# Moving the decay and value loads of units 5 to 11 from SP's queue to GpSimd's, with newly ordered engines

## The chip, the cores and the metric

The kernel runs on one core of one Trainium2 chip. The metric is the device time in microseconds (us) of one execution; the figure quoted is the median over runs. A core has five engines with an in-order instruction queue each: TensorE (PE, matmuls), VectorE (DVE), ScalarE (ACT), GpSimd (POOL) and SyncE (SP, which here only issues DMA transfers). Sixteen DMA engines move the data that the queues of SP and GpSimd ask for.

## The reference

A gated linear attention with a state per head, followed by a dense block with squared ReLU (cut to what matters):

```python
# q, k, v, alpha: (B=4, H=8, S=768, D=48) float32; alpha in [0.8, 1.0)
state = zeros(B, H, D, D)
for t in range(S):
    state = alpha[:, :, t, :, None] * state + einsum('bhd,bhe->bhde', k[:, :, t], v[:, :, t])
    y[:, :, t] = einsum('bhd,bhde->bhe', q[:, :, t], state)
x = y.transpose(0, 2, 1, 3).reshape(3072, 384)
h = x @ w_in                  # (384, 2048)
g = maximum(h, 0) ** 2
out = g @ w_out               # (2048, 384), float32
```

## The kernel before

**Tiling.** The 768 steps of each of the 4 sequences are cut into chunks of T = 256 tokens. A *unit* g is one chunk of one sequence; there are 12, ordered chunk by chunk (units 0 to 3 are the first chunks of the four sequences, 4 to 7 the second, 8 to 11 the last). A chunk's 256 tokens lie on 128 partitions, two neighbouring tokens (j = 0, 1) in a row.

**One unit's steps**, by the names that the order tables use:

- `lda ldk ldq ldv`: four loads of 384 KB (decay alpha, keys, queries, values) into one of four RAW slots (g mod 4); a load waits until the readers of the slot's part have finished with the unit four before.
- `pr` (product of the two tokens' decays, tile prd), `ln` (its logarithm, tile lab), `m1i` (TensorE: running sums over the tokens), `ei` and `ea` (exponentials for keys, ek, and queries, eq), `ec` (decay of the whole chunk, acm), `bk` (the keys' factor of the first token). For units 2 and 3, `m1s`, `es` and `aq` give the queries' factor of the first token; from unit 4 on `lm` (a logarithm of alpha), `lb` (a difference) and `es` do.
- `ekm`, `eqm0`, `eqm1`: keys and queries times their factors (tile qks). `vc`: values cast to bf16 (tile vbf).
- `tr0`, `tr1`: transposes of qks into kqt, on TensorE with copies `et0`, `et1` for units 0 to 2, as DMA transposes issued by SP from unit 3 on.
- `p0`: scores and the new state on TensorE; `mk0`, `mk1` mask the scores (tile pm); `sa`, `sc`, `sd` update the state; `y`: the unit's output; `xe`, `xf` copy it out of PSUM (xbf); `xt` transposes it (TensorE for units 0 to 3, a DMA transpose from SP from unit 4 on).
- Dense block: `s1_g_u` (u = 0 to 7, each 6 matmuls of 256 columns: two pieces of the hidden layer), `re` (ReLU into rr), `sq` (square into gt), `s2_g_j_n` (4 matmuls of 384 columns, n = 0 to 3, for the tokens j), `oe` (copy out of PSUM), `out` (store from SP).
- `win0/1`, `wout0/1`: the weights, loaded by GpSimd's queue at the start. In TensorE's table `+512` and `+256` are filler matmuls on zeros ahead of the first dense work.

**What sets the order.** Nothing is decided while the kernel runs. TABLES holds, for each engine, the complete order of its steps as text; `arrange` assigns each named step to the engine in whose table it stands (many steps can run on two engines, given as `alts`), and `place` puts in the semaphore waits that the dependences need. An engine works its list strictly in order: a step that waits holds all behind it. The same holds for the DMA issues, which stand as steps in the lists of SP and GpSimd. The priorities, costs and due times (FRONT, ATTN, DENSE, P) in the code went into the search that made the tables; in the run they set nothing.

**Around the change.** `load(g)` (line 445) makes the four loads of a unit. POOL_LOADS (line 313) names the loads that go through GpSimd's queue; the rest go through SP's. AFTER (line 1060) holds the loads of the start back: lda2 waits for ldv1, wout0 for ldv1, the loads of unit 3 for wout0.

```python
if nm in POOL_LOADS.get(g, ""):
    ring, cost = "pool", 930
...
load_op[g, nm] = add(ring, lambda e, dst=dst, src=src: e.dma_start(dst, src), cost, ...,
    writes=[key], name=f"ld{nm}{g}", dma=f"{nm}{r}{ring}", lag=1230,
    after=([load_op[gate]] if gate else []))
```

The semaphore of a load is named by kind, slot and ring. Two first-layer groups share two PSUM banks in turn, so that `s1_g_u` waits for the `re` of two groups before; the second layer has one bank, so that the groups of one j wait for the `oe` of the other.

Of the kernel before, what the change touches and what calls it, by code (L numbers as in the profile page):

```python
# [204 lines left out]

TABLES = {
    "act": """
        table ln0_0 ln1_0 ei0_0 xcaus ea0_0 ei1_0 ea1_0 ec1_0 et00_0 ec0_0 vc0 ln1 et01_0 et11_0 ei1 ea1 xe0 xv0
        ec1 vc1 sa1 re0_0 re0_1 sq0_1 re0_3 xe1 re0_4 re0_5 ln2 re0_6 sq0_6 ei2 ea2 ec2 vc2 re1_2 es2 re1_3
        re1_4 et0_2 sq1_3 re1_6 sa2 sq1_6 oe0_0 ln3 ei3 ea3 ec3 oe0_1 es3 xf2 xe2 lm4 ln4 vc3 ei4 ea4 ec4 re2_0  # L210
        re2_1 es4 oe1_0 re2_2 re2_3 re2_4 re2_5 sa3 sq2_5 lm5 re2_7 ln5 re2_6 xe3 ei5 ea5 ec5 xv3 es5 oe2_0
        re3_0 oe2_1 lm6 re3_1 xe4 ln6 re3_4 re3_3 ei6 ea6 ec6 re3_6 sq3_5 re3_7 sq3_7 es6 re4_0 re4_1 re4_2
        re4_3 vc6 xe5 lm7 ln7 re4_7 oe3_1 re4_4 ei7 ea7 ec7 re4_6 sq4_6 es7 oe4_0 re5_0 re5_1 lm8 ln8 xe6 re5_2
        re5_3 ei8 ea8 re5_4 re5_5 es8 re5_6 re5_7 sq5_7 re6_0 re6_1 re6_2 vc8 oe5_0 xe7 lm9 ln9 re6_5 re6_6
        oe5_1 re6_7 ei9 ea9 es9 oe6_0 vc9 re7_0 lm10 re7_1 ln10 xe8 re7_3 ei10 ea10 re7_4 re7_5 es10 re7_6 re7_7
        re8_0 oe7_0 re8_1 re8_2 lm11 ln11 xe9 re8_3 re8_4 ei11 ea11 re8_5 re8_6 sq8_5 es11 sq8_7 re9_0 oe8_0
        vc11 re9_1 oe8_1 xe10 re9_3 re9_4 re9_5 re9_6 re9_7 re10_0 oe9_0 re10_1 re10_2 xe11 oe9_1 re10_3 re10_4
# [4 lines left out]
        zero zlinc zlstr zident zcaus zcaus1 zla0 zla1 zones zown zown0 zown1 zqk0 zqk1 zqk2 zlb0 zlb1 ekm0_0
        eqm0_0 ekm1_0 eqm1_0 et10_0 mk0_0 sa0 mk1_0 ekm1 eqm0_1 eqm1_1 sc0 et0_1 et1_1 mk1_1 mk0_1 sc1 re0_2 xf1
        sq0_3 pr2 xv1 sq0_5 re0_7 re1_0 re1_1 ekm2 sq0_7 aq2 eqm0_2 eqm1_2 re1_5 et1_2 sq1_1 sq1_5 re1_7 mk1_2
        pr3 sq1_7 sc2 mk0_2 bk3 eqm1_3 ekm3 aq3 pr4 eqm0_3 xv2 bk4 lb4 ekm4 eqm1_4 eqm0_4 sq2_1 mk1_3 mk0_3 sc3
        oe1_1 sd3 sq2_7 sq2_6 xf3 lb5 ekm5 eqm1_5 eqm0_5 sa4 mk1_4 mk0_4 re3_2 pr6 sc4 sq3_1 xf4 sq3_3 re3_5
        sq3_6 lb6 ekm6 sa5 mk0_5 sc5 mk1_5 eqm0_6 eqm1_6 oe3_0 xf5 sq4_1 re4_5 pr7 sq4_3 sq4_7 sq4_5 bk7 lb7
        eqm0_7 sa6 eqm1_7 ekm7 sc6 sd6 mk0_6 mk1_6 pr8 oe4_1 xf6 sq5_3 bk8 lb8 ekm8 sq5_5 sq5_6 sa7 mk0_7 sc7
        mk1_7 eqm0_8 eqm1_8 sq6_1 re6_3 sd7 sq6_3 pr9 xf7 re6_4 sq6_5 sq6_6 sq6_7 bk9 lb9 ekm9 eqm0_9 eqm1_9
        mk0_8 sa8 mk1_8 oe6_1 pr10 sq7_1 xf8 re7_2 sq7_3 bk10 lb10 sq7_5 ekm10 sq7_6 sq7_7 sa9 mk0_9 eqm0_10  # L230
# [6 lines left out]
        +256 +256 tr01_0 p0_0 tr11_0 kv0 +512 +512 +512 +256 +256 p1_0 m11 +512 +256 y0 +512 +512 +256 tr0_1 xt0
        tr1_1 +512 +512 +512 +512 +512 +256 p0_1 s1_0_0 s1_0_1 s1_0_3 s1_0_2 y1 s1_0_4 s1_0_5 xt1 s1_0_6 s1_0_7
        m1i2 s1_1_0 s1_1_1 s1_1_2 m1s2 s1_1_3 s1_1_4 tr0_2 s1_1_6 s1_1_5 tr1_2 s2_0_0_0 s1_1_7 p0_2 s2_0_0_1
        s2_0_0_2 s2_0_0_3 s2_0_1_0 s2_0_1_1 m1i3 s2_0_1_2 s2_0_1_3 m1s3 y2 s2_1_0_0 s2_1_0_1 xt2 s2_1_0_2 m1i4  # L240
        s1_2_0 s1_2_1 s2_1_0_3 s1_2_2 s1_2_3 s2_1_1_0 s1_2_4 s2_1_1_1 s1_2_5 p0_3 s2_1_1_2 s1_2_6 s1_2_7
        s2_1_1_3 y3 m1i5 s2_2_0_0 s2_2_0_1 xt3 s2_2_0_2 s2_2_0_3 s1_3_0 p0_4 s2_2_1_0 s2_2_1_1 s2_2_1_2 s2_2_1_3
        s1_3_2 s1_3_1 y4 s1_3_4 s1_3_3 m1i6 s1_3_6 s1_3_5 s2_3_0_0 s2_3_0_1 s1_3_7 p0_5 s2_3_0_2 s1_4_0 s1_4_1
        s2_3_0_3 s1_4_2 s1_4_3 y5 s2_3_1_0 s1_4_5 s2_3_1_1 s2_3_1_2 s1_4_7 s2_3_1_3 s1_4_4 m1i7 s2_4_0_0 s1_4_6
        s2_4_0_1 s2_4_0_2 p0_6 s2_4_0_3 s1_5_1 s1_5_0 s2_4_1_0 s2_4_1_1 s1_5_2 s2_4_1_2 s2_4_1_3 y6 s1_5_3 m1i8
        s2_5_0_0 s1_5_4 s1_5_5 s2_5_0_1 s1_5_6 s1_5_7 p0_7 s2_5_0_2 s1_6_0 s1_6_1 s2_5_0_3 s1_6_2 s1_6_3 y7
        s1_6_4 s2_5_1_0 s2_5_1_1 s1_6_5 s2_5_1_2 s1_6_6 s2_5_1_3 s1_6_7 m1i9 s2_6_0_0 s2_6_0_1 s2_6_0_2 s2_6_0_3
        s1_7_0 p0_8 s2_6_1_0 s2_6_1_1 s2_6_1_2 s2_6_1_3 s1_7_1 y8 s1_7_2 s1_7_3 m1i10 s2_7_0_0 s1_7_4 s1_7_5
        s2_7_0_1 s1_7_6 s1_7_7 s2_7_0_2 p0_9 s2_7_0_3 s1_8_0 s1_8_1 s1_8_2 s2_7_1_0 s2_7_1_1 s2_7_1_2 s2_7_1_3
        y9 m1i11 s1_8_3 s1_8_4 s2_8_0_0 s1_8_5 s1_8_6 s2_8_0_1 s1_8_7 p0_10 s2_8_0_2 s1_9_0 s2_8_0_3 s1_9_1  # L250
        s1_9_2 s2_8_1_0 s2_8_1_1 s2_8_1_2 y10 s2_8_1_3 s1_9_3 s1_9_4 s2_9_0_0 s1_9_5 s1_9_6 s2_9_0_1 s1_9_7
# [863 lines left out]
```

## Time and profile before

| | before |
|---|---|
| median of 3 runs | 174.28 us (173.72 to 176.34) |
| span of the profiled execution, first to last instruction | 171.8 us |
| TensorE matmuls, weight loads | 165.6 us (96%), 128.9 us (75%) |
| VectorE, ScalarE, GpSimd busy | 118.2 us (69%), 108.9 us (63%), 24.2 us (14%) |
| granted TensorE clock | 1.000 |
| DMA packets, bytes | 74743, 33.37 MB (194 GB/s over the span) |
| queue of SP (q1) and of GpSimd (q0), share of 16 engines | 73.6%, 12.4% |

The page gives no device time of the profiled execution other than its span; the median of the runs stands 2.5 us above it. Busy time of TensorE is modelled: matmuls are pipelined, and a busy TensorE can still be waiting between them. DMA issues do not count as busy time of the engine that issues them. A "busy tenths" row cuts the span into 40 slices of 4.3 us, one digit each.

### The profile page before, as it was taken

How to read it: one execution, taken by the hardware profiler on the slowest of the kernel's cores; microseconds unless marked ns; L12 is line 12 of the kernel's file. 1: busy time of each engine (PE TensorE's matmuls, PEld its weight loads, DVE VectorE, ACT ScalarE, POOL GpSimd, SP SyncE). 2: the span in 40 equal slices, each digit the busy share in tenths (PEclk: the TensorE clock that was granted, in tenths of full speed). 3: DMA queues.
4: the chain of work that ended last, by engine and by line, in shares of the span. 5: the costliest groups of instructions: out<-in, count | busy, mean ns of one | idle time of the engine just before them, and what ended most of it. 6: DMA issues, size and time to landing. Idle time of an engine off the chain costs nothing.

```text
span 171.8 us, 5397 instructions
## 1 busy us (share of the span) xinstructions
PE 165.6 (96%) x2377; PEld 128.9 (75%) x2377; DVE 118.2 (69%) x207; ACT 108.9 (63%) x210; POOL 24.2 (14%) x33
## 2 busy tenths in 40 slices
PE   7999999999999999999999999999999999999994
PEld 2556989766877787886768886787788788788773
DVE  5578789888756788975948986887959737432130
ACT  2958689658868278677359567475667464466440
POOL 4052712010252032100240000000420000000000
PEclk9999999999999999999999999999999999999999
DMA  5999999999999999998999998999999582050012
GB/s 143 323 298 186 260 316 219 245 245 288 182 234 209 269 173 211 305 217 146 288 168 211 267 192 153 337 178 243 255 211 205 81 103 85 0 141 0 22 69 92
DMA packets 74743, 33.37 MB, mean 194 GB/s; under 512 B 71648, under 2 KB 71904, under 8 KB 74720
## 3 DMA queue, kind: packets, MB, share of 16 engines
q1 hardware_dynamic: 73184, 28.32, 73.6%
q0 software_dynamic: 1536, 4.72, 12.4%
q8 instruction: 18, 0.29, 0.7%
q14 instruction: 5, 0.04, 0.1%
...
## 4 chain that ended last, share of the span: by engine, by line
PE 58%; DMA 20%; SPq 7%; DVE 6%; ACT 4%; POOL 2%; issue 2%; DVEq 0%
PE psWH L989 25%; PE psO L1035 24%; DMA raw<-in_alpha_dram 7%; DMA wout<-in_moe_w_out_dram 6%; DMA raw<-in_q_dram 4%; SPq L460 3%; DMA raw<-in_k_dram 3%; SPq L654 3%; PE psX L950 2%; POOL raw L460 2%; DVE pm L891 1%; PE psZ L762 1%; PE psX L874 1%; DVE qks L638 1%; DVE qks L643 1%
## 5 line engine op out<-in xcount | busy, mean ns | idle before, releaser
L989 PE MATMUL psWH<-xt,win 128*128 128x256 bf16 x552 | 70.9, 274 | 0.4 <-ACT rr L997 0.3
L989 PEld LDWEIGHTS psWH<-xt,win 128*128 128x128 bf16 x552 | 63.2, 144 | 5.2 <-ACT rr L997 1.1
L1035 PE MATMUL psO<-wout,gt 128*128 128x384 bf16 x352 | 66.7, 326 | 0.0
L997 ACT ACTIVATE rr<-psWH 128x512 bf16<-128x512 f32 x79 | 46.8, 597 | 24.4 <-PE psWH L989 22.9
L1035 PEld LDWEIGHTS psO<-wout,gt 128*128 128x128 bf16 x352 | 32.7, 98 | 16.7 <-DMA wout<-in_moe_w_out_dram 0.2
L1007 DVE TENSOR_TENSOR gt<-rr 128x1024 bf16<-128x1024 bf16 (+1 forms) x46 | 26.6, 584 | 22.0 <-ACT rr L997 21.9
L891 DVE TENSOR_TENSOR pm<-psZ,caus 128x1024 bf16<-128x1024 f32 x12 | 14.6, 1218 | 4.7 <-PE psWH L727 4.1
L1042 ACT ACTIVATE osb<-psO 128x384 f32<-128x384 f32 x17 | 8.3, 491 | 11.7 <-PE psO L1035 11.3
L891 DVE TENSOR_TENSOR pm<-psX,caus 128x1024 bf16<-128x1024 f32 x12 | 14.6, 1218 | 1.0 <-PE psX L874 0.5
L1010 POOL TENSOR_TENSOR gt<-rr 128x1024 bf16<-128x1024 bf16 x3 | 5.7, 1894 | 58.7 <-ACT rr L997 58.7
L643 DVE TENSOR_TENSOR qks<-raw,ek 128x768 bf16<-128x768 f32 x11 | 10.5, 952 | 3.0 <-DMA raw<-in_k_dram 2.5
L638 DVE TENSOR_TENSOR qks<-raw,eq 128x384 bf16<-128x384 f32 x22 | 11.4, 553 | 1.7 <-ACT eq L613 1.0
L1083 PE MATMUL psO<-zero 128*128 128x512 bf16 (+1 forms) x33 | 9.1, 407 | 1.3 <-DVE zero L382 1.3
L999 DVE TENSOR_SCALAR rr<-psWH 128x512 bf16<-128x512 f32 x13 | 8.9, 687 | 1.6 <-PE psWH L989 1.4
L1011 ACT ACTIVATE gt<-rr 128x512 bf16<-128x512 bf16 (+1 forms) x11 | 9.1, 823 | 0.7 <-DVE rr L999 0.4
L910 DVE CAST xbf<-psZ 128x384 bf16<-128x384 f32 x10 | 5.5, 554 | 3.2 <-PE psZ L754 3.2
L634 ACT ACTIVATE vbf<-raw 128x768 bf16<-128x768 f32 x7 | 5.9, 843 | 2.2 <-DMA raw<-in_v_dram 2.1
L567 DVE TENSOR_TENSOR prd<-raw 128x384 f32<-128x384 f32 x9 | 5.7, 636 | 2.1 <-DMA raw<-in_alpha_dram 2.0
L609 ACT ACTIVATE la<-raw 128x384 f32<-128x384 f32 x8 | 4.2, 524 | 4.5 <-DMA raw<-in_alpha_dram 4.5
L570 ACT ACTIVATE lab<-prd 128x384 bf16<-128x384 f32 x10 | 5.2, 521 | 2.4 <-DVE prd L567 2.3
L847 POOL TENSOR_TENSOR sbd<-tmp,acm 128x192 bf16<-128x192 f32 x5 | 2.9, 583 | 25.8 <-DVE tmp L837 22.7
L908 ACT ACTIVATE xbf<-psX 128x384 bf16<-128x384 f32 x11 | 5.3, 482 | 1.9 <-PE psZ L754 1.9
...
## 6 DMA issues: line engine op xcount, KB each, us to landing
raw<-in_alpha_dram SPq DMA_DIRECT2D x11, 384.0 KB, 5.9
raw<-in_k_dram SPq DMA_DIRECT2D x11, 384.0 KB, 5.8
raw<-in_q_dram SPq DMA_DIRECT2D x11, 384.0 KB, 5.0
raw<-in_v_dram SPq DMA_DIRECT2D x11, 384.0 KB, 5.0
out_dram<-osb SPq DMA_DIRECT2D x11, 384.0 KB, 3.4
win<-in_moe_w_in_dram POOLq DMA_DIRECT2D x2, 768.0 KB, 9.9
wout<-in_moe_w_out_dram POOLq DMA_DIRECT2D x2, 768.0 KB, 11.6
raw<-in_alpha_dram POOLq DMA_DIRECT2D x1, 384.0 KB, 11.1
```

What stands on the lines that cost most here:

```text
L460: load_op[g, nm] = add(ring, lambda e, dst=dst, src=src: e.dma_start(dst, src), cost, (L_PRIO[g] + j if ring == "sp" else W_PRIO[2] + 10 * ...
L638: add("dve", lambda e, j=j, dst=dst: e.tensor_tensor(dst, RAW[r][:, 2, :, j, :].rearrange("p (n x) d -> p n x d", x=2), EQ[la][:, j].rearr ...
L643: add("dve", lambda e, a=a, E=E: e.tensor_tensor(QKS[qs][:, a, :, :, 0:D], RAW[r][:, 1 + a].rearrange("p h j d -> p j h d"), E[la][:].rear ...
L891: add("dve", lambda e, hf=hf, psT=psT: e.tensor_tensor(PM[pm][:, hf].rearrange("p r n j t -> p (r n) (j t)"), psT[:, :, :].rearrange("p r ...
L989: ins = pe.matmul(psN[:, i * T:(i + 1) * T], WIN[:, kk, hidden(fj)], mov, start=(kk == 0), stop=(kk == KT - 1))
L997: add("act", lambda e, psN=psN, rr=rr: e.activation(rr, psN, AF.Relu), act_ns(512), pu + 600, reads=[keyN], writes=[("rr", rb, half)], nam ...
L999: alts={"dve": (lambda e, psN=psN, rr=rr: e.tensor_scalar(rr, psN, 0.0, None, ALU.max), dve_ns(512))})
L1007: add("dve", lambda e, dst=dst, sq=sq: e.tensor_tensor(dst, sq, sq, ALU.mult), 148 + k * 267, pu + 1200, reads=[("rr", rb, h) for h in ran ...
L1011: "act": (lambda e, dst=dst, sq=sq: e.activation(dst, sq, AF.Square), act_ns(k * 512))})
L1035: ins = pe.matmul(psS, GT[gt][:, fj, j, :], WOUT[:, fj, :], start=(fj == 0), stop=(fj == FT - 1))
L1042: add("act", lambda e, j=j, psS=psS: e.activation(OSB[ob][:, j], psS, AF.Copy), act_ns(DM), ps_ + 700, reads=[keyS], writes=[("osb", ob, j ...
L1083: pr.arrange(TABLES, lambda n: lambda pe: pe.matmul(psO[:, 0:n], ZERO[:, 0:128], ZERO[:, 0:n], skip_group_check=True), zero)
```

## The change

Loads of decays (a) and values (v) of units 5 to 11, 14 transfers of 384 KB, move from SP's list to GpSimd's. Keys and queries stay on SP. All five order tables are new. GpSimd's list grows from 29 to 59 steps, SP's shrinks from 84 to 70, ScalarE's from 210 to 193; VectorE's goes from 206 to 207 and TensorE's keeps its 276. Between the engines, 43 steps go from ScalarE to VectorE and 32 the other way (ReLUs, squares, copies out of PSUM), 18 from VectorE to GpSimd (pr2, pr3, pr4, pr6, pr8, pr10, pr11, bk3, bk8, bk9, bk11, aq3, sd3, sd7 and the squares sq1_5, sq7_5, sq10_3, sq11_3) and 8 back, 8 from ScalarE to GpSimd (vc1, vc3, vc6, vc9, vc11, sq0_6, sq2_5, sq8_5) and 2 back. No computation is added or removed.

```diff
-    POOL_LOADS = {2: "akqv"}
+    POOL_LOADS = {2: 'akqv', 5: 'av', 6: 'av', 7: 'av', 8: 'av', 9: 'av', 10: 'av', 11: 'av'}
```

The whole lists of GpSimd and SP, and of the others the parts that the text speaks of ("..." marks what is left out):

```diff
     "act": """
-        ... oe0_0 ln3 ei3 ea3 ec3 oe0_1 es3 xf2 xe2 lm4 ln4 vc3 ei4 ea4 ec4 ...
+        ... ln3 oe0_0 ei3 ea3 ec3 sq1_7 es3 lm4 xv2 ln4 oe0_1 ei4 re2_1 ea4 ec4 re2_3 vc5 es4 ...
     "dve": """
-        ... ekm2 sq0_7 aq2 eqm0_2 eqm1_2 re1_5 et1_2 ... pr3 sq1_7 sc2 mk0_2 bk3 eqm1_3 ekm3 aq3 pr4 eqm0_3 xv2 bk4 ...
+        ... ekm2 sq0_5 sq0_7 aq2 eqm0_2 eqm1_2 et0_2 re1_6 et1_2 re1_7 mk1_2 mk0_2 sc2 sq1_6 xe2 xf2 eqm0_3 eqm1_3 ekm3 re2_0 bk4 ...
-        ... xf5 sq4_1 re4_5 pr7 sq4_3 sq4_7 sq4_5 bk7 lb7 eqm0_7 sa6 eqm1_7 ekm7 ...
+        ... eqm0_6 sd5 eqm1_6 sq4_3 re4_5 pr9 lb7 bk7 sq4_5 re4_7 eqm1_7 ekm7 sa6 mk1_6 sc6 mk0_6 eqm0_7 ...
     "pe": """
-        ... s2_4_0_1 s2_4_0_2 p0_6 ... y6 s1_5_3 m1i8 ...
+        ... y4 m1i6 s1_3_4 s1_3_5 s2_3_0_0 s1_3_6 s1_3_7 s2_3_0_1 p0_5 s2_3_0_2 s2_3_0_3 s1_4_1 m1i7 s1_4_0 s1_4_3 y5
+        s2_3_1_0 s1_4_2 s2_3_1_1 s1_4_5 s2_3_1_2 s2_3_1_3 s1_4_4 s1_4_7 s2_4_0_0 s1_4_6 s2_4_0_1 s2_4_0_2 p0_6 ...
     "pool": """
-        slinc slstr sident scaus scaus1 win0 win1 lda2 sd0 ldq2 ldv2 ldk2 wout0 sd1 wout1 bk2 sd2 sq2_3 vc4 pr5
-        bk5 sd4 vc5 bk6 sd5 sq5_1 vc7 sq8_1 vc10
+        slinc sident scaus1 scaus slstr win0 win1 lda2 ldv2 vc1 ldk2 wout0 ldq2 sd0 pr2 wout1 sq0_6 sq1_5 ldv5
+        pr3 pr4 bk3 aq3 vc3 lda5 pr5 sq2_5 sd3 lda6 bk5 lda7 pr6 bk6 ldv6 lda8 vc6 pr8 lda9 lda11 lda10 ldv7 vc7
+        pr10 ldv8 bk8 pr11 bk9 ldv9 ldv10 ldv11 sd7 vc9 vc10 sq7_5 bk11 sq8_5 vc11 sq10_3 sq11_3
     "sp": """
-        lda0 ldk0 ldq0 ldv0 lda1 ldk1 ldv1 ldq1 lda3 ldk3 ldq3 lda4 ldv3 ldk4 ldq4 ldv4 tr0_3 tr1_3 lda5 tr0_4
-        out0_1 tr1_4 ldk5 ldq5 ldv5 lda6 ldk6 tr1_5 tr0_5 out2_1 xt4 ldq6 out1_1 ldv6 lda7 ldq7 ldk7 tr0_6 tr1_6
-        xt5 ldv7 out3_1 lda8 ldk8 tr0_7 tr1_7 out4_1 xt6 ldq8 ldv8 lda9 ldq9 ldk9 tr0_8 tr1_8 xt7 ldv9 lda10
-        out5_1 ldk10 tr0_9 tr1_9 out6_1 xt8 ldq10 ldv10 lda11 ldk11 tr0_10 tr1_10 out7_1 xt9 ldq11 ldv11 tr0_11
-        tr1_11 xt10 out8_1 xt11 out9_1 out10_1 out11_0 out11_10 out11_11
+        lda0 ldk0 ldq0 ldv0 lda1 ldk1 ldq1 ldv1 lda3 lda4 ldq3 ldk3 ldk4 ldv3 ldq4 tr1_3 tr0_3 ldk5 ldv4 tr0_4
+        tr1_4 out0_1 ldq5 ldk6 tr0_5 tr1_5 out1_1 xt4 ldq6 ldk7 ldq7 tr1_6 tr0_6 xt5 out2_1 ldk8 tr1_7 xt6 tr0_7
+        ldq8 out3_1 ldk9 ldq9 out4_1 tr1_8 xt7 tr0_8 ldk10 ldq10 out5_1 tr1_9 tr0_9 xt8 out6_1 ldk11 ldq11
+        tr0_10 tr1_10 xt9 tr1_11 out7_1 tr0_11 xt10 xt11 out9_1 out8_1 out11_0 out10_1 out11_10 out11_11
```

More of the change, by code (lines that the diff above doesn't have):

```diff
@@ L207 @@
     "act": """
[L208 to L217, printed above, removed]
@@ L220 @@
+        xe11 re10_3 re10_5 re10_4 re10_7 re10_6 re11_0 sq11_1 oe10_0 re11_2 oe10_1 re11_5 sq11_5 re11_7 oe11_0
+        oe11_11
     """,
     "dve": """
[L222 to L230, printed above, removed]
@@ L237 @@
[L237 to L246, printed above, removed]
@@ L247 @@
[L247 to L251, printed above, removed]
```

51 lines of the change are left out of this document (41 added, 10 removed).

## The prediction

> **What bounds the kernel now.** I read the busy times and the slices of the page first, then the chain of waits, then the timelines of TensorE, GpSimd and VectorE at the places that the change touches.
>
> ```profile
> span 171.8 us, 5397 instructions
> PE 165.6 (96%) x2377; PEld 128.9 (75%) x2377; DVE 118.2 (69%) x207; ACT 108.9 (63%) x210; POOL 24.2 (14%) x33
> PEclk9999999999999999999999999999999999999999
> DMA  5999999999999999998999998999999582050012
> ```
>
> TensorE is nearly never idle and its granted clock is full. The 16 DMA engines are as full as TensorE until slice 31 of 40 (about 130 us) and then nearly empty, so the first three quarters are a race of two full resources; GpSimd has 86% of its time free. A busy TensorE may still run with waits between pipelined matmuls, so I count its work. The dense layers, with the chain's pieces as their pace:
>
> ```profile
> L989 PE MATMUL psWH<-xt,win x552: 272/273/334, 18.1 to 164.6; 128*128 128x256 bf16 x184
> L1035 PE MATMUL psO<-wout,gt x352: 323/326/337, 30.9 to 166.5; 128*128 128x384 bf16 x176
> ```
>
> ```profile
> 81.29 6.32 DMA raw<-in_alpha_dram
> 87.62 0.57 DVE prd L567
> 88.22 0.53 ACT lab L570
> ...
> 91.20 0.65 PE psO L1035 x4
> 91.85 1.31 PE psWH L989 x12
> ...
> 166.81 2.65 PE psX L950 x32
> ```
>
> Undisturbed, a first-layer matmul takes 1.31/12 = 0.109 us and a second-layer one 0.65/4 = 0.163 us. By the code there are 576 of the one (12 units of 8 groups of 6) and 368 of the other ahead of the last 32: 62.9 + 59.8 + 2.65 = 125.4 us. TensorE's work runs from 18.1 us (first row, its first dense matmul) to 166.81 + 2.65 = 169.5 us, so 26.0 us are left for attention and waits. What an attention step costs, and what a wait looks like, stand in TensorE's timeline:
>
> ```profile
> 77.40 0.33 PE L576 MATMUL psWH<-lab,linc 128*128 128x384 bf16 x1
> ...
> 77.67 0.81 PE L1035 MATMUL psO<-wout,gt 128*128 128x384 bf16 x4
> ...
> 78.97 1.46 PE L1035 MATMUL psO<-wout,gt 128*128 128x384 bf16 x8
> 80.83 0.42 PE L874 MATMUL psX<-kqt 64*64 64x128 bf16 x16 [0.40 <-ACT eq L613]
> ...
> 81.65 0.82 PE L1035 MATMUL psO<-wout,gt 128*128 128x384 bf16 x4
> ...
> 86.97 0.37 PE L762 MATMUL psZ<-vbf,pm 64*128 64x48 bf16 x16
> ...
> 87.67 0.88 PE L989 MATMUL psWH<-xt,win 128*128 128x256 bf16 x6
> 88.80 0.34 PE L576 MATMUL psWH<-lab,linc 128*128 128x384 bf16 x1 [0.24 <-ACT lab L570]
> ```
>
> Start to start, the decay sums (m1i) take 0.27, the scores (p0) 0.82, the output (y) 0.70 us. After 18.1 us there are 10 m1i, 10 p0 and 11 y: 2.7 + 8.2 + 7.7 = 18.6 us; the 34 transposing matmuls of 128 columns for units 1 to 3 add 34 x 0.055 = 1.9 us (half the pace of 256 columns). So **about 5.5 us of TensorE's time after 18 us is waiting**: all that better orders and earlier loads can win, short of a shorter start. Two of the waits are in the rows: the 8 matmuls at 78.97 would make way at 80.27, and p0 of unit 6 starts at 80.83 (0.56 late, behind its transposes); the 6 at 87.67 would make way at 88.33, and m1i8 comes at 88.80 (0.47 late). The second is a load: the chain rows above show the decay load of unit 8, issued at 81.29, landing at 87.6 and going through prd and lab into that matmul.
>
> **The change, part by part.**
>
> *The start.* The two orders of TensorE hold the same 23 + 10 filler matmuls ahead of s1_0_0, SP's first six loads are the same, and ekm1, eqm, et0_1, et1_1 still gate p0_1. I take 0 (bounds -0.7 to +0.7, one 0.7 us VectorE step put earlier or later; `sc0` now stands ahead of the masks, `eqm0_0` ahead of the keys).
>
> *Queries of unit 2.* On GpSimd's queue the order was lda2, ldq2, ldv2, ldk2, wout0; it becomes lda2, ldv2, vc1, ldk2, wout0, ldq2.
>
> ```profile
> wout<-in_moe_w_out_dram POOLq DMA_DIRECT2D x1, 768.0 KB, 10.9
> ...
> raw<-in_q_dram POOLq DMA_DIRECT2D x1, 384.0 KB, 7.9
> ```
>
> ```profile
> 16.49 0.92 POOL L460 DMA_DIRECT2D raw<-in_q_dram  x1
> ...
> 19.15 0.58 POOL L433 DMA_DIRECT2D wout<-in_moe_w_out_dram  x1
> ...
> 50.61 1.00 POOL L569 TENSOR_TENSOR prd<-raw 128x384 f32<-128x384 f32 x1 [1.87 <-DMA raw<-in_alpha_dram]
> ...
> 122.56 1.89 POOL L1010 TENSOR_TENSOR gt<-rr 128x1024 bf16<-128x1024 bf16 x1 [34.92 <-ACT rr L997]
> ```
>
> ```profile
> 29.15 1.03 DVE L638 TENSOR_TENSOR qks<-raw,eq 128x384 bf16<-128x384 f32 x2
> ...
> 39.86 0.55 DVE L605 TENSOR_TENSOR eq<-eq,raw 128x384 f32<-128x384 f32 x1
> ...
> 40.80 0.55 DVE L638 TENSOR_TENSOR qks<-raw,eq 128x384 bf16<-128x384 f32 x1
> ```
>
> q2 landed at 16.49 + 7.9 = 24.4 and wout0 at 19.15 + 10.9 = 30.1 us. The queue works through the same bytes in order, so q2 now ends where wout0 did, at about 30.2, and its two VectorE products cannot begin at 29.15. They end near 31.3 instead of 30.2, with et0_2 and re1_6 now ahead of et1_2. Late next is p0_2, by 1.1 to 1.8 us, of which the m1 and s2 work ahead of it covers about half: **+0.8** (0 to +1.8). In return SP's loads of units 3 and 4, which wait for wout0, start about 1.1 us sooner.
>
> ```profile
> SPq L460 <- DMA wout<-in_moe_w_out_dram: 20.9, 1, 20.9
> ```
>
> *Unit 3.* pr3, bk3, aq3 move from VectorE to GpSimd: 1.00 us each by the prd row instead of 0.55. VectorE's order becomes eqm0_3, eqm1_3, ekm3, all behind aq3, and es3 stands behind sq1_7 on ScalarE. Before, one eqm (0.55) stood between aq3 and the transposes; now two eqm and ekm (0.55 + 0.55 + 0.95). With the slower aq3 (0.45) and sq1_7 (0.6) the transposes are issued some 2.5 us later than the 41.38 here:
>
> ```profile
> 41.38 4.00 SPq L654 DMA_TRANSPOSE kqt<-qks  x2
> ```
>
> Those 4.00 us are SP held by a full queue; with one load fewer ahead it is held a load's 1.2 us less. What is left, 1.3 us, is late at p0_3, and re2_0, queued behind eqm0_3's wait, holds a PSUM bank that s1_2_2 needs: **+1.0** (0 to +2.5).
>
> *Decay loads of 4 to 11, and transposes.* lda4 is second in SP's order, and lda5 to lda11 go to GpSimd, so the waits of m1i4 and m1i8 should go.
>
> ```profile
> PE psWH L576 <- ACT lab L570: 0.4, 2, 0.2
> ```
>
> These are the two; start to start each cost about 0.45. Transposes no longer stand behind the a and v loads on SP: half of p0_6's 0.56 goes, and some 0.5 elsewhere: **-1.7** (0 to -4.2; the bound leaves 1.3 of the 5.5, for hitches of 0.1 that no load explains).
>
> *The loads as GpSimd sees them.* Each load occupies GpSimd 0.92 us, 14 x 0.9 = 13 us: nothing by itself, since it was 14% busy, but its queue is in order and its loads now stand between steps that wait. The tight place is unit 6 to 9: `bk6 ldv6 lda8 vc6 pr8 lda9`, while VectorE has `re4_5 pr9 lb7 bk7 sq4_5`: pr9 waits for lda9's data, and lb7, bk7 and sq4_5 queue behind it, for which es7, lda11 and s2_4_0_2 wait. Durations, from VectorE's timeline:
>
> ```profile
> 74.34 0.69 DVE L999 TENSOR_SCALAR rr<-psWH 128x512 bf16<-128x512 f32 x1 [0.26 <-PE psWH L989]
> 74.95 0.55 DVE L567 TENSOR_TENSOR prd<-raw 128x384 f32<-128x384 f32 x1
> ...
> 78.23 0.69 DVE L1007 TENSOR_TENSOR gt<-rr 128x1024 bf16<-128x1024 bf16 x1 [0.88 <-ACT rr L997]
> 78.84 0.55 DVE L596 TENSOR_TENSOR ek<-ek,raw 128x384 f32<-128x384 f32 x1
> 79.31 0.55 DVE L611 TENSOR_TENSOR la<-psWH,la 128x384 f32<-128x384 f32 x1
> ```
>
> From m1i6's start: the sums 0.4, ei6 0.5, bk6 1.0, ldv6 0.9, so lda8 is issued at +2.8; with L from issue to landing, pr8 ends at 3.8 + L and a9 is there at 3.8 + 2L. TensorE reaches s1_4_5 after 8 first-layer and 6 second-layer groups, p0_5, y5 and two m1i: 14 x 0.655 + 0.82 + 0.70 + 0.54 = +11.2; then 0.82 and re4_5 put VectorE at pr9 at +12.7. s2_4_0_2, which needs sq4_5, comes 8 groups after s1_4_5's start, at +16.4; after pr9, lb7, bk7, sq4_5 (2.3 us) sq4_5 would be ready at +15.0, so 1.4 us are to spare. VectorE waits if L exceeds 4.45, TensorE if it exceeds 5.15.
>
> ```profile
> DMA to landing us min/median/max: 3.5/5.5/11.1
> ```
>
> With the median L of 5.5 the wait is 2.1 and TensorE loses **+0.7** (0 at L = 3.5; 5.5 at the 7.9 of ldq2).
>
> *Two engines on one memory port.* GpSimd's arithmetic steps on SBUF go from 16 to 32.
>
> ```profile
> 123.58 1.30 DVE L567 TENSOR_TENSOR prd<-raw 128x384 f32<-128x384 f32 x1 [0.41 <-DMA raw<-in_alpha_dram]
> ```
>
> ```profile
> L567 DVE TENSOR_TENSOR prd<-raw x9: 548/554/1297, 23.2 to 123.6; 128x384 f32<-128x384 f32 x9
> ```
>
> The product at 123.58 ran beside the GpSimd step of 122.56 and took 0.74 us longer than its fellows: one strong case in 16 steps. Three of them in 32, a third of it reaching TensorE: **+0.8** (0 to +2.2, if all three do).
>
> **Sum:** 0 + 0.8 + 1.0 - 1.7 + 0.7 + 0.8 = +1.6 us on the profiled 171.8, a span of 173.4. The median of the runs, 174.28, stands 2.5 us above the profiled span; carried over: **175.9 us**, own range 173.5 to 178.5.
>
> **Rivals.**
>
> *GpSimd's queue sets the pace* (slower). Place: lda8, pr8, lda9 ahead of VectorE's pr9; it decides from L = 5.15 on. For it: L counts twice in series, and ldq2 took 7.9 on this queue. Against: that one stood behind weights. At L = 7.9, a9 is there at +19.6, VectorE waits 6.9 and TensorE 5.5 instead of 0.7: 180.7 us.
>
> *Waits vanish* (faster). All steps meet in time, the losses stay 0, and 4.2 of the 5.5 us go: 170.1 us. For it: GpSimd's idle time, and SP's blocked issues. Against: the waits are many small ones on transposes and masks, not on loads.
>
> *The loads move and nothing comes sooner.* The DMA row is full until 130 us; a load issued earlier queues in the engines instead of on SP, and gains and losses cancel: 174.3 us. The Trainium skill, page "DMA: Bandwidth & Descriptors", section "Issuing engines are not separate DMA queues", says that transfers of all issuing engines share the same 16 engines and that a second issuer saves only issue time; by that rule this rival is the outcome. The full DMA row agrees, but here SP's issue itself holds 4.00 us of transposes.
>
> *The port.* If every overlap costs, not one in 16: VectorE's steps with two SBUF inputs fill about a third of the span, so about 11 of the 32 GpSimd steps meet one, at half of 0.74 each 4 us on VectorE, two thirds on TensorE: 2.7 us more than none, 1.9 more than taken: 177.8 us. The Trainium skill, page "SBUF — State Buffer", section "Who interferes with whom", says just this: a VectorE instruction with two SBUF inputs and a GpSimd one that reads SBUF block each other entirely. The row at 123.58 agrees for one pair.
>
> **How the numbers follow.** Forecast 0.45, GpSimd's queue 0.22, waits vanish 0.13, nothing sooner 0.10, port 0.10. The bound of 2% (3.5 us: 170.8 and 177.8) is about what a measurement of this kernel can tell from no change. Faster: the third case but for 0.01, and 0.01 of the forecast's lower tail, 0.13. Slower: 0.21 of the second, 0.06 of the port, 0.12 of the forecast's upper part, 0.39. Within: 0.48. The range goes from 170.8 to 181.0: it leaves out most of the third case and the second's upper end, under 2 in 10.
>
> **What would show it.** Right: ldq2 landing at or after 30 us, the transposes of unit 3 issued near 43.5, m1i8 without a wait, a VectorE wait of about 2 us on the decay DMA near 76 to 79 us, prd or qks steps of over 0.9 us, dense work still from 18.1 us on. Wrong: a9 there before re4_5 ends, TensorE's waits below 3 us in all, or a start shifted by over 1 us.

## The result, and the profile after

The changed kernel takes 186.32 us in the median of five runs (183.43 to 197.20), the kernel before on the same chip 174.26 us (173.72 to 176.34). In three of the five executions the mean granted clock was lower (0.956 to 0.982) and the time longer than in the other two, 183.43 and 185.46 us; by these two the ratio is 1.059, 95% interval 1.050 to 1.068: slower by about 6%. The profiled execution took 185.46 us, 183.9 of it the span. Line numbers are one lower than before.

The page of the changed kernel: span, TensorE's busy time, the granted clock and the load of the DMA engines in 40 slices.

```profile
span 183.9 us, 5400 instructions
PE 166.5 (90%) x2377; PEld 130.2 (71%) x2377; DVE 124.9 (68%) x208; ACT 100.0 (54%) x193; POOL 56.0 (30%) x63
...
PEclk9999999999999999889999999999999999999999
DMA  5999999999899899966896989998947176042004
```

TensorE's busy time is nearly the same (165.6 before), its share fell from 96% to 90%: it waits. The DMA row, solid before, has gaps in the middle, and just there two slices of the clock row fall to 8. TensorE's dense matmuls by line (first and last start at the end of the numbers) begin at 19.4 us instead of 18.1:

```profile
L988 PE MATMUL psWH<-xt,win x552: 272/273/421, 19.4 to 176.5; 128*128 128x256 bf16 x184
```

TensorE's waits (total, times, longest):

```profile
PE psWH L988 <- DMA xt<-xbf: 6.2, 2, 4.7
PE psX L873 <- DMA kqt<-qks: 2.5, 2, 1.4
...
PE psO L1034 <- ACT osb L1041: 1.1, 1, 1.1
```

None of these three is a wait of over 0.2 us before; DMA transposes on SP (L931 xt, the normalized activations; L653 kqt, keys and queries) now make up 8.7 us. The chain of waits shows the two longest hold-ups:

```profile
67.38 8.92 DMA xt<-xbf
76.31 0.05 issue
76.35 1.48 PE psWH L988 x6
...
88.14 6.13 DMA out_dram<-osb
...
94.35 0.50 ACT osb L1041
```

xt4 took 8.92 us from issue to landing. The landings of all eight xt transposes by DMA, of after and then of before:

```profile
DMA to landing us min/median/max: 2.7/3.4/8.9
```

```profile
DMA to landing us min/median/max: 2.7/3.2/3.7
```

What was in flight beside xt4: SP's timeline, then GpSimd's.

```profile
67.38 1.25 SPq L931 DMA_TRANSPOSE xt<-xbf  x1
68.68 0.58 SPq L459 DMA_DIRECT2D raw<-in_q_dram  x1
```

```profile
66.99 0.93 POOL L459 DMA_DIRECT2D raw<-in_v_dram  x1
67.90 0.88 POOL L459 DMA_DIRECT2D raw<-in_alpha_dram  x1
```

Two of the loads that the change moved, ldv6 and lda8, were issued 0.39 us before xt4 and 0.52 us behind it. Before, these bytes stood behind xt4 in SP's own queue. The stretch 67 to 77 us by the DMA view (40 slices of 0.25 us; a queue's packets, MB, share of the 16 engines):

```profile
DMA  9999999829464699999978899999999000299999
GB/s 150 157 127 276 406 319 381 246 17 186 34 84 84 204 382 380 295 454 234 196 248 275 228 238 155 110 130 106 60 36 30 2 9 9 51 326 195 327 324 320
...
q8 instruction: 1, 0.02, 0.9%
```

From 74 us on (slice 29) the sixteen engines move 60 GB/s and less, for 0.75 us next to nothing, while TensorE still waits for xt4's last packets. One transfer of instructions (16 KB) falls into the stretch too, from 73.5 us on. And the wait is paid for once more, as the granted clock shows (the last number but two of a row):

```profile
67.00:74.00 7.00, 4.63 (x91) 3.28 (x89) 6.10 (x9) 4.00 (x8) 2.61 (x4) 1.00 1.03 218
74.00:80.00 6.00, 3.65 (x21) 2.90 (x22) 0.39 (x1) 1.80 (x4) 1.88 (x2) 0.72 1.23 222
```

The 0.72 is a mean: by the trace's clock records the clock is at 0.50 from 76.47 us on, for 3.41 us, and at 1.00 before and after. The six matmuls at 76.35 took 1.48 us instead of 0.65.

*Where the 12.1 us of span went.* I took the start-to-start time of every named step of TensorE and subtracted the median of its kind; what is left are its waits. The dense work starts 1.3 us later (19.42 against 18.14). The waits sum to 16.4 us against 6.25 before, 10.1 more. The tail behind the last group of dense matmuls is 0.2 longer, 0.5 is spread. The large ones among the 16.4: xt4 4.9, and 1.8 of half clock and hitches behind it; xt5 1.7; four waits for kqt 4.4; the result buffers at 88 to 94 us 1.1.

### The profile page after: what moved, and what is told of

The parts are those of the page before. It is cut to its first block, busy times and chain, and to the rows that moved or that the text cites. A ratio compares the mean times of both kernels' runs of the same rounds, so it can differ in the third digit from the quotient of the medians.

```text
span 183.9 us, 5400 instructions
## 1 busy us (share of the span) xinstructions
PE 166.5 (90%) x2377; PEld 130.2 (71%) x2377; DVE 124.9 (68%) x208; ACT 100.0 (54%) x193; POOL 56.0 (30%) x63
## 4 chain that ended last, share of the span: by engine, by line
PE 68%; DMA 17%; DVE 8%; SPq 3%; issue 2%; ACT 1%; POOL 1%; DVEq 0%; ACTq 0%
PE psWH L988 28%; PE psO L1034 24%; DMA kqt<-qks 6%; DMA xt<-xbf 5%; DMA out_dram<-osb 3%; DMA raw<-in_q_dram 3%; PE psX L873 2%; DVE qks L637 2%; PE psZ L761 2%; SPq L931 2%; PE psX L949 1%; PE psO L988 1%; PE psWH L575 1%; PE psX L761 1%; PE psWH L726 1%
## 5 line engine op out<-in xcount | busy, mean ns | idle before, releaser
L996 ACT ACTIVATE rr<-psWH 128x512 bf16<-128x512 f32 x57 | 33.8, 596 | 32.5 <-PE psWH L988 31.9
L998 DVE TENSOR_SCALAR rr<-psWH 128x512 bf16<-128x512 f32 x35 | 23.9, 687 | 20.0 <-PE psWH L988 19.8
L1009 POOL TENSOR_TENSOR gt<-rr 128x1024 bf16<-128x1024 bf16 (+1 forms) x7 | 12.6, 1803 | 47.7 <-ACT rr L996 32.7
L1006 DVE TENSOR_TENSOR gt<-rr 128x1024 bf16<-128x1024 bf16 (+1 forms) x33 | 21.0, 652 | 4.9 <-ACT rr L996 4.6
L1010 ACT ACTIVATE gt<-rr 128x1024 bf16<-128x1024 bf16 (+1 forms) x20 | 16.9, 862 | 2.6 <-DVE rr L998 2.2
L568 POOL TENSOR_TENSOR prd<-raw 128x384 f32<-128x384 f32 x8 | 8.4, 1048 | 14.8 <-DMA raw<-in_alpha_dram 14.5
L593 POOL TENSOR_TENSOR ek<-ek,raw 128x384 f32<-128x384 f32 x6 | 6.1, 1009 | 19.9 <-ACT ek L586 19.9
L632 POOL CAST vbf<-raw 128x768 bf16<-128x768 f32 x7 | 6.2, 879 | 15.7 <-DMA raw<-in_v_dram 15.7
L459 POOL DMA_DIRECT2D raw<-in_alpha_dram x8 | 7.3, 910 | 11.0 <-DVE ek L595 9.0
L873 PE MATMUL psX<-kqt 64*64 64x128 bf16 x192 | 5.0, 221 | 4.3 <-DMA kqt<-qks 2.5
```

The costliest lines, as they stand in the source:

```text
L873: ins = pe.matmul(psT[64 * c:64 * c + 64, rr_, o:o + 128], keys, mov)
L996: add("act", lambda e, psN=psN, rr=rr: e.activation(rr, psN, AF.Relu), act_ns(512), pu + 600, reads=[keyN], writes=[("rr", rb, half)], nam ...
L998: alts={"dve": (lambda e, psN=psN, rr=rr: e.tensor_scalar(rr, psN, 0.0, None, ALU.max), dve_ns(512))})
L1006: add("dve", lambda e, dst=dst, sq=sq: e.tensor_tensor(dst, sq, sq, ALU.mult), 148 + k * 267, pu + 1200, reads=[("rr", rb, h) for h in ran ...
L1009: alts={"pool": (lambda e, dst=dst, sq=sq: e.tensor_tensor(dst, sq, sq, ALU.mult), 200 + k * 840), "act": (lambda e, dst=dst, sq=sq: e.act ...
L1010: "act": (lambda e, dst=dst, sq=sq: e.activation(dst, sq, AF.Square), act_ns(k * 512))})
```

## Experiments

**1. Which half of the change costs.** Loads only: the orders of before, the 14 loads taken from SP's list and put into GpSimd's. Orders only: the orders of after, the 14 loads put back into SP's list near the places where they were issued (ldv6 and lda8, for one, right behind xt4).

```diff
 # loads only, GpSimd's list of before
-sd2 sq2_3 vc4 pr5 bk5 sd4 vc5 bk6 sd5 sq5_1 vc7 sq8_1 vc10
+sd2 sq2_3 lda5 vc4 pr5 ldv5 bk5 lda6 sd4 vc5 bk6 ldv6 lda7 sd5 ldv7 lda8 sq5_1 vc7 ldv8 lda9 ldv9
+lda10 ldv10 lda11 sq8_1 vc10 ldv11
```

> The orders of the kernel before, with only the 14 loads moved to GpSimd's list. Theory (a DMA transpose that runs beside a load of GpSimd's queue takes 5 to 9 us instead of 3 to 4.5, and TensorE and SP wait behind it): slower, 178 to 184 us, with transposes above 5 us wherever such a load is in flight. Rival (the new orders of the engines are at fault, the queue is harmless): 173.5 to 175.5 us.

> The new orders of all engines, with the 14 loads back in SP's list near the places where they were issued. Theory: 174 to 178 us (about 1.3 us for the later start and 1 to 2 us for unit 3 remain), xt4 lands in under 4.5 us. Rival (the orders): 182 to 186 us, the same waits at s1_4_0 and s1_5_0.

Before took 172.30 us there. Loads only: 186.72 us (185.86 to 187.91), ratio 1.084 [1.078, 1.091]. Orders only: 180.16 us (179.86 to 180.74), ratio 1.047 [1.042, 1.051]. Both cost, and each more than I expected; they do not add (14.4 and 7.9 us against 12.1); that with the new orders other loads meet other transposes is my reading of it. In the kernel of the loads alone one transpose carries most of it. Its chain, then its windows, then GpSimd's timeline:

```profile
91.53 12.36 DMA xt<-xbf
...
104.02 2.75 PE psWH L989 x12
```

```profile
97.00:104.00 7.00, 0.47 (x3) 0.09 (x2) 2.67 (x4) 0.09 (x1) 0.00 (x0) 0.81 0.99 218
104.00:108.00 4.00, 3.98 (x17) 2.80 (x18) 0.00 (x0) 1.19 (x2) 0.00 (x0) 0.50 1.04 300
```

```profile
91.08 0.93 POOL L460 DMA_DIRECT2D raw<-in_v_dram  x1
...
95.50 0.88 POOL L460 DMA_DIRECT2D raw<-in_alpha_dram  x1
```

Six loads in a row leave GpSimd, the first 0.45 us ahead of xt6 and the others while it is out. It takes 12.36 us, TensorE stands 6.55 us, and then runs four microseconds at a granted clock of 0.50: 12 matmuls in 2.75 us instead of 1.31.

**2. Take the loads out of a transpose's way.** In the changed kernel ldv6 and lda8 go back to SP, right behind xt4; in the kernel of the loads alone the seven loads from ldv8 on go back to SP.

```diff
 # changed kernel
-POOL: ... bk6 ldv6 lda8 vc6 ...        SP: ... xt4 ldq6 ldk7 ...
+POOL: ... bk6 vc6 ...                  SP: ... xt4 ldv6 lda8 ldq6 ldk7 ...
```

> The changed kernel, with two loads alone (values of unit 6, decays of unit 8) issued by SP right behind xt4 instead of by GpSimd beside it. Theory: xt4 lands 3 to 4 us after its issue instead of 8.9, the 4.9 us wait of s1_4_0 goes, 178 to 181.5 us. Rival (the DMA engines are full of bytes then, from whichever queue): xt4 still takes 6 us or more, 184 to 187 us.

> The kernel before with only lda5 to lda8 and ldv5 to ldv7 moved to GpSimd, in the places they had in the kernel of the loads alone (186.7 us); the seven later loads stay with SP. Theory (the burst of six GpSimd loads issued 91.1 to 95.5 us held xt6 for 12.4 us, TensorE waited 6.7 us and ran its next steps at half its clock, some 2 us): xt6 back near 3 us, no wait over 3 us, 8 to 10 us less: 177 to 179 us. Rival (GpSimd's order or the queue's longer road costs a little at every load, spread over the span): half of it at most, 181 to 184 us.

The first: 182.63 us (180.36 to 184.96), ratio 1.051 [1.044, 1.058]; xt4 is back at 3.15 us and the profiled span is 3.9 us shorter, but xt5, with lda11, lda10 and ldv7 beside it, takes 6.3 (5.9 in the changed kernel). The median lies above the 178 to 181.5 us that I expected, and the interval overlaps that of the changed kernel (1.050 to 1.068), so that the gain is seen in the profiled executions and not in the times. The second: 176.96 us (175.79 to 177.97), ratio 1.024 [1.017, 1.031], 9.8 us less than with all fourteen, as the theory said; xt6 takes 3.1 us. Its kqt transposes

```profile
DMA to landing us min/median/max: 3.6/4.7/9.4
```

show that a long transpose costs nothing where TensorE comes later still: the 9.4 is tr0_6, issued 0.64 us behind lda8 and 1.55 behind ldv7, and TensorE comes to its product only 2.6 us after it has landed. What is left of the loss are other waits:

```profile
PE psWH L575 <- ACT lab L569: 2.8, 1, 2.8
PE psZ L753 <- issue: 1.8, 1, 1.8
```

The first is lda5, late on GpSimd's queue. In the second nothing that the profile shows was waited for: TensorE stops in the middle of y5's matmuls, as its timeline has it,

```profile
74.35 0.18 PE L753 MATMUL psZ<-sbd,kqt 64*128 64x48 bf16 x1
76.38 0.18 PE L753 MATMUL psZ<-smd,kqt 64*128 64x48 bf16 x1 [1.85 <-issue]
```

with an instruction transfer in flight from 74.0 to 75.1 us. That it lacked instructions is my inference. It then lost 1.7 us more at half clock (0.50 for 3.41 us).

The longest xt transpose (us) sets the kernels with twelve or fourteen of the loads on GpSimd apart from the others:

| kernel | a and v loads of units 5 to 11 | longest xt |
|---|---|---|
| before | SP | 3.7 |
| orders only | SP | 4.2 |
| stores sooner; stores and cast mended (below) | SP | 4.3; 4.3 |
| SP's new list alone (below) | SP | 3.5 |
| seven loads back on SP | 7 on GpSimd | 4.2 |
| after | GpSimd | 8.9 |
| loads only | GpSimd | 12.4 |
| cast back (below) | GpSimd | 6.4 |
| xt4 free | 12 on GpSimd | 6.3 |
| three mends (below) | 12 on GpSimd | 7.9 |

**3. The transpose by itself.** Three small kernels issue one transpose of xt's size in company, one case after the other, each waiting for the last. In the names of the cases t is the transpose, o a store and s a load of 384 KB, all three issued by SP; p is the same load by GpSimd, a by ScalarE; w is a weight load of 768 KB by GpSimd. The names tell what was in company, not what left first: GpSimd's loads go out one every 0.9 to 1.1 us, the first of them between 0.5 us ahead of the transpose and 0.5 us behind it.

> The disputed cost alone; the attention and the dense block are left out and zeros are stored. In turn: a transposing DMA of the size of xt alone; one and two 384-KB loads on GpSimd's queue, with and without it; the same on ScalarE's queue; the load on SP ahead of it or behind it; a 768-KB weight load in 3-KB runs on GpSimd's queue beside it. Theory: alone 2.7 us, beside one GpSimd load 5 us, beside two 8 us; behind or ahead of an SP load 3 to 4.5 us. Of its two forms, 'any second queue' puts ScalarE's loads at the same 5 and 8 us, 'the software queue alone' at under 4.5 us. Rival (only the bytes count): about 1.2 us more per load from whichever queue.

> Attention and dense block are left out, zeros are stored: single DMAs timed on an idle core, in cases one after the other. Alone, a transpose of xt's size took 2.75 us and beside one or two GpSimd loads of 384 KB 4.1 to 4.4 us. Here a store is issued ahead of it, as in the kernel, so that the loads are ahead of it too. Theory (packets of all queues share the sixteen engines in turn, so the transpose ends when about as many bytes as were in flight at its issue have gone by): store and transpose 3 to 4 us from the transpose's issue; with one GpSimd load ahead 4.5 to 5.5, with two 5.5 to 6.5, with six 9 to 12 us, and three SP loads behind it add under 1 us; six SP loads behind it add nothing. Six ScalarE loads beside it hold it as six of GpSimd do, 9 to 13 us. Rival (it is special to GpSimd's queue): six ScalarE loads leave it under 6 us. Rival (it is not the DMAs but what the engines do beside them): six GpSimd loads hold it for under 7 us.

> Attention and dense block are left out, zeros are stored: the transposes in a crowd again, now with TensorE running 1800 matmuls beside them, so that its instructions are fetched in 16-KB transfers by the same DMA engines (in the whole kernels one of these, 0.9 to 1.9 us long, comes every 8 to 10 us). On the idle core the transpose took 2.8 to 3.0 us behind a store and 5.2 to 6.0 us beside two to six GpSimd loads, not the 8.2 to 12.4 us of the whole kernels. Theory (a fetch on one DMA engine holds the last packets of a transpose that shares it, most of all beside GpSimd loads): transposes with a fetch in flight are 1 to 2 us longer without GpSimd loads (4 to 5 us) and 7 to 10 us beside them; those without a fetch as on the idle core. Rival (work of the engines in general slows the DMAs): all cases beside GpSimd loads are longer than 6.5 us, fetch or not. Rival (neither): 5.2 to 6.0 us whether or not a fetch falls in, and the long ones of the whole kernels stay open.

From issue to landing of the transpose, from the traces (us):

```
first kernel              t 2.74 to 2.82   ts 2.73, 2.77   st 3.91, 4.09
                          tp 4.31, 4.44    tpp 4.07, 4.39  ta 4.30, 4.33   taa 5.72, 5.87
                          tw 5.23, 5.52
second, store ahead       ot 3.04          otssssss 2.80
                          pot 4.78, 4.83   potp 5.42, 5.47   potpsss 5.24, 5.57
                          ppppppot 5.95    ppppppotsss 5.16, 5.29   aaaaaaot 5.58
third, TensorE busy       no GpSimd load: 2.77 to 3.19, with a fetch 3.15 and 3.47
                          beside 2 to 4 GpSimd loads, no 16-KB fetch or only its edge: 4.91 to 5.45 (8)
                          the same, a 16-KB fetch inside: 6.43, 6.73, 7.37, 8.03
```

Read in three steps. On SP alone, what is queued behind a transpose does not touch it (2.80 with six loads behind). A load from another queue does: its packets go through the same sixteen engines, and the transpose takes 4.1 to 6.0 us. That is not a property of GpSimd's queue, for ScalarE's loads do the same (5.7 to 5.9 with two, 5.6 with six). And it hardly grows with the crowd: I had expected 8 us beside two GpSimd loads and 9 to 12 beside six, and 4.1 to 4.4 (with a store ahead 5.2 to 5.6) and 5.2 to 6.0 came out; but of six loads at these intervals only the first two left within 1 us of the transpose. I looked for the missing part in the instruction transfers. TensorE's program comes in by the same engines; the pages of all whole kernels show this queue:

```profile
q8 instruction: 18, 0.29, 0.6%
```

0.29 MB in 18 transfers is 16 KB each, and in the traces one takes 0.9 to 1.9 us. Where one fell inside a transpose beside GpSimd loads in the third kernel, the transpose took 1.0 to 2.6 us more than the longest without; where there were no such loads, 0.3 more at most. In one of the four, the 6.73, the transfer began only 5.85 us after the transpose's issue, when it had already outlasted all eight without one. So the theory holds in direction, with 6.4 to 8.0 us for the 7 to 10 I expected, on three cases. In the whole kernels such a transfer seems to count without GpSimd loads too: in the kernel after, tr1_6 and tr1_11 met no load, and took 3.71 us and, with a transfer inside and a store behind, 5.84. In the kernel before, the nine kqt transposes with the most of such a transfer inside took 5.3 us on average, the other nine 4.0; but the four longest of the nine also stood behind three loads of SP still in flight.

The longest ones it does not explain. In xt6 of loads only (12.36) the transfer began 10.1 us after the issue, in xt4 of after (8.92) 6.2 us, and xt5 of the three mends (below) took 7.91 us with none in flight. The packets in the traces show another difference. The pages of before and then of after, queue of SP (q1) and of GpSimd (q0), packets and MB:

```profile
q1 hardware_dynamic: 73184, 28.32, 73.6%
q0 software_dynamic: 1536, 4.72, 12.4%
```

```profile
q1 hardware_dynamic: 58624, 22.81, 58.0%
q0 software_dynamic: 3104, 10.23, 21.9%
```

A moved load leaves SP's queue as 1040 packets and comes back in GpSimd's as 112, most of them of 4224 bytes; one of these takes 0.2 us as a rule and up to 2.5 us in a crowd, one of the 768 packets of 256 bytes of an xt transpose 0.02 us. In the small kernel with six GpSimd loads (5.95 us) the transpose's packets start between 75.78 and 77.26 us and the loads' from 76.89 on: the transpose is nearly through when they come. With xt6 of loads only the loads' packets start at 93.23 us, ahead of the transpose's, which start one by one between them from 94.07 to 101.77. In xt5 of the three mends they mix too. Where the loads' first packets come 0.2 to 0.4 us before the transpose's last, it takes 5 to 6 us: in the kernel with the cast back (below) the same two loads left 0.14 and 1.06 us behind xt4, instead of 0.39 ahead and 0.52 behind, and it took 5.33 us instead of 8.92; xt5 of the kernel with xt4 free took 6.29. So the mixing of the packets fits the long ones. But one case of the third small kernel has it and took 4.91 us, and no small kernel sent its loads well ahead of the transpose: it is not tested, and the cause of the last microseconds stays open.

**4. The orders.** ScalarE waits for stores in the kernel of the orders alone, and TensorE for ScalarE; before has neither. ScalarE's row, then TensorE's:

```profile
ACT osb L1041 <- DMA out_dram<-osb: 9.0, 3, 4.2
```

```profile
PE psO L1034 <- ACT osb L1041: 2.8, 2, 1.7
```

There are two result buffers; out0_1, out1_1 and out2_1 stand behind transposes and loads in SP's new list, so the copies of two units later (oe2_0, oe4_0) find the buffer taken. I moved the stores one or two places up, and then vc1 back to ScalarE:

```diff
 # orders only, SP's list
-tr1_3 tr0_3 lda5 ... tr1_4 lda6 out0_1 ldq5 ... tr1_5 out1_1 xt4 ... xt5 out2_1 ... ldv8 out3_1
+tr1_3 tr0_3 out0_1 lda5 ... tr1_4 out1_1 lda6 ldq5 ... tr1_5 out2_1 xt4 ... xt5 out3_1 ... ldv8
 # then, besides
-POOL: ... ldv2 vc1 ldk2 ...    ACT: ... ea1 xe0 ...
+POOL: ... ldv2 ldk2 ...        ACT: ... ea1 vc1 xe0 ...
```

> The new orders with all loads of units 5 to 11 on SP (the kernel of the orders alone, 180.2 us), and the stores of results of units 0 to 3 each issued one or two places sooner in SP's list: behind tr0_3, tr1_4, tr1_5 and xt5. Theory (with only two result buffers, the late stores hold ScalarE's copies oe2_0 and oe4_0, and so TensorE): in the kernel of the orders alone TensorE waits 2.8 us for ScalarE's osb and ScalarE 9.0 us for the stores; both near 0 here, and 2 to 3 us less, 177 to 178.5 us. Rival (the copies are late anyway because of the order of their engine, the store is only the last of several): waits move to other steps, under 1 us gained, 179.3 to 180.5 us.

> As the run before, and the cast vc1 from GpSimd back to ScalarE, behind ea1. Theory (GpSimd's cast beside VectorE's eqm1_1 and eqm0_1 doubles both, 1.2 us each in place of 0.55): these two back at 0.55 to 0.6 us, dense work from about 18.2 us in place of 19.1, 0.9 to 1.1 us less than the kernel with the stores alone. Rival (the start is late because of the order ekm, eqm and kv on VectorE and TensorE): the steps get short but dense work still starts after 18.8 us, under 0.4 us gained.

Stores: 178.73 us (177.55 to 180.74), ratio 1.032 [1.026, 1.039]. Both waits are gone from the trace. Above before it stands 6.2 us by the medians, instead of 7.9: 1.7 us gained, a little under the 2 to 3 that I expected (2.5 by the ratios). With the cast: 177.33 us (176.92 to 177.98), ratio 1.025 [1.020, 1.031]; the intervals of the two overlap, so what the cast gives can't be told from these times. The trace of the changed kernel with the cast alone moved tells more:

> The changed kernel with the cast vc1 moved from GpSimd back to ScalarE, behind ea1; nothing else. Theory (GpSimd's cast beside them makes VectorE's eqm1_1 and eqm0_1 1.2 us each in place of 0.55, and this is what puts off the dense work): both steps near 0.55 us, the stretch from p1_0 to the first dense matmul 6.7 to 7.0 us in place of 7.63, 0.5 to 1.2 us less than the changed kernel. Rival (the order of the other engines sets the start, and the cast on ScalarE makes ea1's followers later): the stretch stays over 7.3 us and the time within 0.4 us.

VectorE's two products eqm1_1 and eqm0_1, in the kernel before, after, and after with the cast back:

```profile
14.29 1.02 DVE L638 TENSOR_TENSOR qks<-raw,eq 128x384 bf16<-128x384 f32 x2
```

```profile
14.40 2.27 DVE L637 TENSOR_TENSOR qks<-raw,eq 128x384 bf16<-128x384 f32 x2
```

```profile
14.03 1.02 DVE L637 TENSOR_TENSOR qks<-raw,eq 128x384 bf16<-128x384 f32 x2
```

and what GpSimd did in the middle case:

```profile
15.23 1.02 POOL L632 CAST vbf<-raw 128x768 bf16<-128x768 f32 x1
```

The pair costs 1.25 us more beside the cast, and with the cast away the first dense matmul comes at 18.18 us instead of 19.42:

```profile
18.18 1.15 PE L988 MATMUL psWH<-xt,win 128*128 128x256 bf16 x9
```

That is the whole shift of the start. The times of that kernel, 180.98 to 190.31 us (median 186.32, ratio 1.066 [1.056, 1.076]), spread too far to show 1.2 us.

> The changed kernel with ldv6 and lda8 issued by SP behind xt4, the stores of units 0 to 3 sooner in SP's list and vc1 on ScalarE; twelve loads stay with GpSimd. Theory (the terms are separate and add): the kernel with xt4 free took 182.6 us; stores and cast gave 2.8 us in the kernel of the orders; so 179 to 180.5 us, which is 2 to 3 us above the same kernel with all loads on SP (177.3 us): what the twelve loads left still cost, seen at xt5 (over 5 us) and at tr0_8 (over 5.5 us). Rival (the waits behind the transposes take up whatever the other mends free): 181.5 to 182.5 us.

All three mends in the changed kernel, twelve loads left with GpSimd: four executions of 180.34 to 187.10 us, median 184.32. The lowest equals that of xt4's mend alone (180.36), the median is above its 182.63; only the lowest lies in the 179 to 180.5 that I expected. So the times don't show that the terms add, and are too wide to show that they don't. In the profiled execution xt5 took 7.9 us, and TensorE waited 3.7 us for it.

> The kernel before with SP's list alone replaced by the one of the kernel of the orders alone (all loads of units 5 to 11 on SP, stores late, transposes in the new order); the lists of the other four engines as before. It splits the 8 us of the orders alone (180.2 us). Theory (it is mostly SP's order: late stores hold the copies out of the two result buffers, and loads and transposes come in an order that suits other engines' lists): 177 to 180 us, with a wait of ScalarE or VectorE for stores of results of several us. Rival (it is the order of the computing engines): 172.5 to 175 us, and no wait for stores that reaches TensorE.

178.12 us (176.91 to 179.38), ratio 1.034 [1.026, 1.042]: the number I expected, but not for my reason. ScalarE waits only 0.3 us for stores. TensorE's longest waits, then GpSimd's timeline:

```profile
PE psWH L575 <- ACT lab L569: 3.0, 2, 2.6
PE psO L1034 <- DVE osb L1043: 1.5, 1, 1.5
```

```profile
52.08 0.93 POOL L632 CAST vbf<-raw 128x768 bf16<-128x768 f32 x1 [4.16 <-DMA raw<-in_v_dram]
52.97 1.17 POOL L568 TENSOR_TENSOR prd<-raw 128x384 f32<-128x384 f32 x1
```

GpSimd stands 4.16 us at vc4, whose load the new SP list brings late, and pr5, lab and m1i5 queue behind it. VectorE's osb in the second row stood behind a wait of 1.68 us for the queries of unit 6, which come late too. The run shows that a list of SP made for other lists costs 5.8 us, not that this list costs it in the changed kernel. Of the 7.9 us of the orders alone, stores and cast make up 3.1. The other 4.8 are spread over waits of 0.3 to 1.3 us, in the kernel with both mended for instance

```profile
PE psX L873 <- issue: 1.4, 3, 0.9
...
PE psX L925 <- ACT xbf L907: 1.0, 1, 1.0
PE psWH L988 <- DVE rr L998: 0.8, 2, 0.5
PE psO L1034 <- DVE gt L1006: 0.7, 1, 0.7
```

and no run here takes these apart. No version beat the kernel before.

## Why the prediction was wrong, point by point

The forecast was 175.9 us, the range up to 181.0; 186.3 came out. The sign of the sum was right (+1.6 us; measured by the medians, 12.1), its size by a factor of seven wrong, and the sign is partly luck: of the terms that made it positive only unit 3 and the port were paid, the port at the start, where I had put 0.

- **Decay loads and transposes, -1.7: the step that failed.** Its first half came true: m1i4 and m1i8 no longer wait for decays. For the other half I wrote that transposes no longer stand behind the a and v loads on SP, and counted a gain. They do not stand behind them; they share the engines with them. In one queue a load ahead of a transpose delays it by some 1.2 us and one behind it not at all; a load from a second queue makes 2.8 us into 4.1 to 6.0, and up to 12.4 in the whole kernels. Measured: waits for xt and kqt of 8.7 us where I had a gain of 0.8, none of that size before. The row that could have told me was in my prediction: the DMA engines 90% busy. I took it as a race that SP's order loses, not as the place where a second queue would push in. The rival that nothing comes sooner was near the truth in its mechanism (the transfers queue in the engines), but it took gains and losses to cancel. The Trainium skill, "DMA: Bandwidth & Descriptors", section "Issuing engines are not separate DMA queues", says that the transfers of all issuers interleave on the same 16 engines; the ScalarE and GpSimd cases (5.6 and 5.2 to 6.0 us) agree. It also says that a second issuer saves only issue time; here it cost.
- **The clock.** A wait had one price in my sum. Behind the wait of 4.7 us the clock stood at 0.50 for 3.4 us (0.72 in the mean over six), with that of 6.55 us for 6.8 us, four of them behind it. The Trainium skill, "TensorE: Matmul & The Clock Gate", section "Part 1: The HAM clock gate (the "warmup" mystery)", has the rule of a half-rate array after idling and some 3.4 us to warm up again; the 3.4 and the four microseconds at 0.50 agree. How long a wait brings it about these runs leave open: in the kernel with seven loads back one of 1.85 us did and one of 2.8 us did not. My sum had no such term.
- **The start, 0 (bounds -0.7 to +0.7): outside.** +1.3 us, for a cause that I had priced elsewhere: the port. vc1 moved to GpSimd beside two VectorE products. I had read vc1 only as a step ahead of ldq2. The term for the port (+0.8, a third of three cases) was of the order of this one case. The Trainium skill's rule in "SBUF — State Buffer", section "Who interferes with whom", that a VectorE instruction with two SBUF inputs and a GpSimd one that reads SBUF exclude each other, agrees: the pair took 1.25 us more beside a cast of 1.02.
- **Result buffers: not in the sum at all.** I went through the loads and transposes of SP's list and not through its stores. 1.1 us of TensorE in the changed kernel, 1.7 us by the experiment in the kernel of the orders alone.
- **The orders as a whole.** With all these loads on SP they still cost 7.9 us, where my terms for them (start, queries of unit 2, unit 3) make 1.8. Stores and cast are 3.1 of it; for the other 4.8 I can name the waits but no cause.
- **Queries of unit 2, +0.8:** ldq2 landed at 30.54 us, as worked out (30.2), and VectorE waited 0.35 us for it; but TensorE has no wait ahead of p0_2 at 33.91 us, so the term was near 0. **Unit 3, +1.0:** its transposes were issued from 43.53 us on (I had put near 43.5), and tr0_3 landed at 50.25 us, for which TensorE waited 1.3 us.
- **The loads as GpSimd sees them, +0.7:** lda8 took 8.21 us, beyond the 5.15 from which pr9 should have held TensorE. It did not: TensorE and with it VectorE were held by xt4 until 76.35, and lda9's data were there at 81.4, ahead of pr9 at 84.5. Counted from m1i6 at 65.08 these data came at +16.3, where I had VectorE at pr9 at +12.7, so without xt4 the place would have held it (worked out, no run shows it). So the rival built on this place also failed, though its time (180.7) was the nearest: the loads' long way hurt the transposes first, not the reader of the loads.
